# Starting the conversion of the second layer's weights at the third expert block instead of the first

## The chip, the core and the metric

One NeuronCore of one Trainium2 chip runs the whole program. The metric is device microseconds (us) of one execution. Engines are named as in the profile: PE is TensorE's matmul (PEld its weight load), DVE is VectorE, ACT is ScalarE, POOL is GpSimd, and SP is SyncE, which only issues transfers here.

## The reference

Three layers follow each other: a windowed attention with sink tokens, a mixture of eight experts, and a dense layer with a rational activation.

```
x = attention(q, k, v)                    # 1536 tokens x 512
for e in range(8):                        # each token goes to its best expert, or to none
    h = max(x[e's tokens] @ w1[e], 0)     # 512 -> 1024
    y[e's tokens] = gate * (h @ w2[e])    # 1024 -> 512
x = x + y
h = x @ w_in                              # 512 -> 2048, w_in in float64
g = (a0 + a1 h + a2 h^2 + a3 h^3) / (1 + |b0| |h| + |b1| h^2 + 1e-6)
out = g @ w_out                           # 2048 -> 512, w_out in float64
```

`w_in` and `w_out` arrive as 64-bit floats, 8 MB each. [...] The text below calls the dense layer "the second layer".

## The kernel before

**Stages.** The attention and the routing take the first 149 us. Then come nine expert blocks, 0 to 8 (eight experts and one spare block), each for up to 128 tokens. Then the second layer runs in 48 steps to the end.

**An expert block.** Block i needs its tokens transposed in SBUF (tile `xbT`, copied by ACT from PSUM, `block_tx_out`, L955) and eight weight chunks of 512 KB (tile `wch`, four of `w1` and four of `w2`). PE multiplies in two halves (`block_g1`, L965), ACT takes the positive part of each half (tile `hT`, L970), PE transposes the next block's tokens (tile `xtr`, L950) and multiplies by `w2` in eight pieces (`block_g2`, L976, sum `yps`). ACT copies the sum out and issues its store (L983, L984). From block 4 on, PE also transposes tokens of the second layer (`ztr`, L1046), which ACT and DVE split into a high and a low part (L1048, L1049).

**Weight chunks and their rooms.** 36 chunks (experts 0 to 3 and half of expert 4) have rooms of their own and are issued before block 1 begins. The chunks after them reuse twelve rooms, so each is issued once PE has used up the chunk that held its room. SP issues all of them (L606, L609) in the order in which the program lists them; an issue that has to wait holds up everything behind it on SP.

**The conversion.** One piece of `w_in` or `w_out` (128x512 values, 512 KB, tile `raw`) passes through these stations, one letter each in the order string:

```python
def conv_load():     # SP: L906, into one of three raw buffers
    sp.dma_start(r.rearrange("p a b -> p (a b)").bitcast(mybir.dt.int64), src)
def conv_word():     # T, DVE: L930, L931, L932, from raw into ta
def conv_hi(eng):    # U, ACT: L912, the high part
    eng.copy(chi[0][1], chi[0][0])
def conv_lo():       # V, DVE: L918, the low part
    dve.tensor_tensor(lo, v_, hi.bitcast(F32), op=ALU.subtract)
def loads_on():      # L
    more_chunks()
    while len(craw) < CRAW and conv_load():    # CRAW = 3 pieces ahead
        pass
```

24 of the 32 pieces (`NCM = 24`) belong to the expert blocks; the other eight are converted in the second layer. From the seventh piece on, a piece goes into a room that an expert's chunk has left.

**Order.** Nothing schedules the work at run time: each engine takes its instructions in program order. `BLOCK` (L72 to L75) is the order of one block. A word is a letter, a piece number and an offset to the block, so that `x01` in block i makes the transposes of block i+1.

```python
BLOCK = """
L2-1 G00 b03 L3-1 a00 o00 T00 U00 G10 V00 L40 x01 a10 T10 U10 F00 L50 F10 X01 V10 T20 U20 F20 F30 V20 L60 T30 U30
F40 F50 V30 z00 F60 F70 y00 L70
"""
```

G and F are PE's two products, a is `hT`, x and X the transposes and their copy, y the output, z the second layer's tokens, L the loads. T, U and V each stand four times, so a block has four places for a conversion. The table `bstep` (L1112 to L1117) maps the letters to functions. After the blocks, a branch over a loop (L1333) leads into the second layer; block 8's second product lies behind it, interleaved with the first steps.

Of the kernel before, what the change touches and what calls it, by code (L numbers as in the profile page):

```python
# [24 lines left out]
T = S // 128  # L25
# [48 lines left out]
F40 F50 V30 z00 F60 F70 y00 L70  # L74
"""  # L75
PO = (6, 12)


def build(nc, tc, q, k, v, n_sink, window, w_skip, w_gate, w1, w2, w_in, w_out, pa, pb, out):
    ctx = ExitStack()  # L80
    with ctx:
        ctx.enter_context(tc.manual_schedule())
        emit(nc, tc, ctx, q, k, v, n_sink, window, w_skip, w_gate, w1, w2, w_in, w_out, pa, pb, out)


def emit(nc, tc, ctx, q, k, v, n_sink, window, w_skip, w_gate, w1, w2, w_in, w_out, pa, pb, out):
    act, dve, pool, pe, sp = nc.scalar, nc.vector, nc.gpsimd, nc.tensor, nc.sync
# [822 lines left out]
    def conv_hi(eng):  # L910
        if chi:
            eng.copy(chi[0][1], chi[0][0])  # L912
            clo.append(chi.pop(0))

    def conv_lo():
        if clo:
            v_, hi, lo, into, key = clo.pop(0)
            dve.tensor_tensor(lo, v_, hi.bitcast(F32), op=ALU.subtract)  # L918
            into[key] = (hi, lo)

    def conv_word():

        if not craw:
            return [lambda: None] * 3
        r, *to = craw.pop(0)
        w0, w1_ = r[:, :, 0], r[:, :, 1]
        ta = stg_now[0].tile([128, 512], I32, tag="ta", name="ta", bufs=3 if stg_now[0] is stg else 2)
        chi.append((ta.bitcast(F32), *to))
        return [
            lambda: dve.tensor_scalar(ta, w1_, 3, 0x3FFFFFFF, op0=ALU.logical_shift_left, op1=ALU.bitwise_and),  # L930
            lambda: dve.scalar_tensor_tensor(ta, w1_, -0x40000000, ta, op0=ALU.bitwise_and, op1=ALU.bitwise_or),  # L931
            lambda: dve.scalar_tensor_tensor(ta, w0, 29, ta, op0=ALU.logical_shift_right, op1=ALU.bitwise_or),  # L932
        ]
# [82 lines left out]
    def place_out(ts):  # L1016

        for t in ts:
            w = scatter(pd[:, :], posi[:, t:t + 1], pk[:, t, :])
            tc.declare_no_dep(w.ins, group="pd", reason="every token has a place of its own")  # L1020
            tc.add_to_no_dep_group("pd", w.ins)
# [41 lines left out]
    def loads_on():  # L1063
        more_chunks()
        while len(craw) < CRAW and conv_load():
            pass

    def at_block(i):

        if i == 0:  # L1070
            flex.append(block_index(flex_sel, exk[:, 0:1], rt, ptr, ""))
        if i < 2:
            place_out(range(PO[0] * i, PO[i]))
        if i == 2:
            place_in()
        if i == 3:
            place_split()
            for t in range(XBUF):
                zx[t] = z_load(t)
# [27 lines left out]
    def step_z(i, n):  # L1107
# [4 lines left out]
    bstep = {  # L1112
        "G": step_G, "a": step_a, "F": step_F, "y": step_y,
        "b": step_b, "x": step_x, "X": step_X, "z": step_z,
        "T": lambda i, n: [op() for op in conv_word()], "U": lambda i, n: conv_hi(act), "V": lambda i, n: conv_lo(),
        "L": lambda i, n: loads_on(), "o": lambda i, n: at_block(i),
    }  # L1117
    made = set()
# [1 line left out]
    for p in range(-1, NBLK + 1):  # L1120
        for w in BLOCK.split():
            o, n, i = w[0], int(w[1]), p + int(w[2:])
# [236 lines left out]
    for w in JOIN.split():  # L1359
        o, n, i = w[0], int(w[1]), int(w[2:])  # L1360
# [17 lines left out]
    for n in range(-2, NS + 8):  # L1378
        for w in STEP.split():
            o, i, t = w[0], int(w[1]), n + int(w[2:])  # L1380
# [100 lines left out]
```

## Time and profile before

| what | value |
|---|---|
| median of 3 runs | 613.36 us (613.06 to 613.96) |
| the profiled execution | 612.33 us, span 610.5 us |
| PE / PEld busy | 537.9 us (88%) / 441.0 us (72%) |
| DVE / ACT / POOL busy | 415.5 / 351.9 / 261.1 us |
| moved by DMA | 86.59 MB, mean 142 GB/s |
| by SP's queue and its like (q1) | 72.75 MB |

The span is what the instructions cover; the profiled execution's own time is 1.83 us longer. Busy time alone doesn't tell what bounds a stage: PE is 88% busy over the whole span, yet there are stretches in which it does nothing. In each row of the timelines below the columns are start, duration, engine, line, operation and tiles, count, and in brackets how long the engine had been idle before and what ended that. SPq and ACTq rows are the issue of a transfer, not its landing.

### The profile page before, as it was taken

How to read it: one execution, taken by the hardware profiler on the slowest of the kernel's cores; microseconds unless marked ns; L12 is line 12 of the kernel's file. 1: busy time of each engine (PE TensorE's matmuls, PEld its weight loads, DVE VectorE, ACT ScalarE, POOL GpSimd, SP SyncE). 2: the span in 40 equal slices, each digit the busy share in tenths (PEclk: the TensorE clock that was granted, in tenths of full speed). 3: DMA queues.
4: the chain of work that ended last, by engine and by line, in shares of the span. 5: the costliest groups of instructions: out<-in, count | busy, mean ns of one | idle time of the engine just before them, and what ended most of it. 6: DMA issues, size and time to landing. Idle time of an engine off the chain costs nothing. (4 is left out here: it accounts for less than half of the span.)

```text
span 610.5 us, 8951 instructions
## 1 busy us (share of the span) xinstructions
PE 537.9 (88%) x2980; PEld 441.0 (72%) x2980; DVE 415.5 (68%) x842; ACT 351.9 (58%) x706; POOL 261.1 (43%) x347
## 2 busy tenths in 40 slices
PE   1899999984909999999699776999999999999993
PEld 1799999973608677777567555787888888888882
DVE  2698899987117277650038999877688776688761
ACT  3799999951003133331145656776777776677761
POOL 3865555325610020100023544766656634754453
PEclk9999999995968999999889999899999999999998
DMA  4929999647987957999302320101100100100001
GB/s 118 208 48 260 274 293 272 237 167 252 304 215 274 367 210 242 383 403 338 124 0 88 103 86 1 52 18 52 71 0 19 51 1 0 70 1 2 0 1 69
DMA packets 78599, 86.59 MB, mean 142 GB/s; under 512 B 43516, under 2 KB 56832, under 8 KB 78544
## 3 DMA queue, kind: packets, MB, share of 16 engines
q1 hardware_dynamic: 73312, 72.75, 38.1%
q0 software_dynamic: 3792, 10.80, 5.7%
q10 hardware_dynamic: 1440, 2.36, 1.0%
q8 instruction: 27, 0.44, 0.3%
q14 instruction: 28, 0.23, 0.1%
HBM read 74.61 MB, written 11.29 MB: 141 GB/s over the span
## 5 line engine op out<-in xcount | busy, mean ns | idle before, releaser
L1181 PE MATMUL hT<-zh,wc 128*128 128x512 f32 x384 | 132.5, 407 | 9.5 <-DMA raw<-in_moe_w_in 5.8
L1233 PE MATMUL acc<-wc,gh 128*128 128x512 f32 x368 | 94.0, 396 | 8.7 <-ACT gh L1201 8.7
L1206 POOL TENSOR_TENSOR w<-w,u 128x512 f32<-128x512 f32 x46 | 63.7, 1385 | 74.7 <-ACT w L1192 73.1
L1181 PEld LDWEIGHTS hT<-zh,wc 128*128 128x128 f32 x384 | 74.2, 193 | 27.0 <-issue 6.5
L1233 PEld LDWEIGHTS acc<-wc,gh 128*128 128x128 f32 x368 | 69.0, 189 | 26.6 <-ACT gh L1201 11.2
L965 PEld LDWEIGHTS hps<-xbT,wch 128*128 128x128 f32 x576 | 71.3, 205 | 21.3 <-ACT xbT L955 18.2
L965 PE MATMUL hps<-xbT,wch 128*128 128x128 f32 x576 | 71.9, 289 | 16.7 <-ACT xbT L955 16.7
L1209 POOL TENSOR_TENSOR gl<-p,gh 128x512 fp32r<-128x512 f32 x46 | 59.8, 1301 | 41.6 <-issue 32.3
L1181 PE MATMUL hT<-zl,wc 128*128 128x512 f32 x192 | 77.0, 401 | 0.4 <-DVE zl L1049 0.4
L912 ACT CAST wc<-ta 128x512 fp32r<-128x512 f32 x32 | 19.8, 618 | 84.2 <-DVE ta L932 72.7
L976 PE MATMUL yps<-wch,hT 128*128 128x512 f32 x144 | 64.5, 594 | 1.4 <-ACT hT L970 1.4
L1219 DVE SCALAR_TENSOR_TENSOR w<-w,cf,u 128x512 f32<-128x512 f32 x46 | 38.4, 834 | 32.2 <-ACT u L1198 32.2
L1233 PE MATMUL acc<-wc,gl 128*128 128x512 f32 x184 | 50.5, 393 | 0.2 <-POOL gl L1209 0.2
L378 ACT ACTIVATE P<-P,rmin 128x260 f32<-128x260 f32 (+1 forms) x96 | 48.6, 513 | 0.2
L1223 DVE SCALAR_TENSOR_TENSOR p<-p,cf,w 128x512 f32<-128x512 f32 x46 | 47.1, 1024 | 1.6
L976 PEld LDWEIGHTS yps<-wch,hT 128*128 128x128 f32 x144 | 26.3, 190 | 29.9 <-issue 26.7
L445 PE MATMUL xps<-P,vph 128*128 128x256 f32 x176 | 46.2, 294 | 0.0
L761 POOL DMA_INDIRECT zx<-xd,tix x12 | 12.9, 1075 | 75.3 <-PE ztr L1046 60.6
L1181 PEld LDWEIGHTS hT<-zl,wc 128*128 128x128 f32 x192 | 37.3, 194 | 9.4 <-DVE zl L1049 0.9
L1201 ACT CAST gh<-p 128x512 fp32r<-128x512 f32 x46 | 28.3, 615 | 26.9 <-DVE p L1223 26.7
L1196 ACT ACTIVATE u<-w,cf 128x512 f32<-128x512 f32 x46 | 33.3, 723 | 16.5 <-POOL w L1206 16.5
L1215 DVE TENSOR_TENSOR p<-p,hT 128x512 f32<-128x512 f32 x46 | 31.4, 682 | 14.2 <-ACT p L1194 14.2
(228 smaller groups left out, 1144.7 us busy)
## 6 DMA issues: line engine op xcount, KB each, us to landing
wch<-in_moe_w SPq DMA_DIRECT2D x72, 512.0 KB
raw<-in_moe_w_in SPq DMA_DIRECT2D x16, 512.0 KB
raw<-in_moe_w_out SPq DMA_DIRECT2D x16, 512.0 KB
kraw<-in_k SPq DMA_DIRECT2D x31, 192.0 KB
qraw<-in_q SPq DMA_DIRECT2D x8, 384.0 KB
vraw<-in_v SPq DMA_DIRECT2D x8, 384.0 KB
xd<-xs SPq DMA_DIRECT2D x16, 192.0 KB
yd<-zero SPq DMA_DIRECT2D x10, 256.0 KB
```

Source lines behind the costliest of these rows:

```text
L378: act.activation(dst, dst, AF.Exp, scale=-1.0, bias=rmin[u][:, t:t + 1], accum_out=ssum[:, u, t:t + 1])
L445: pe.matmul(xps[pr][bank][:, q0:q0 + w], vv, pp, start=(h == 0 and kt in (0, 3) and n == 0), stop=(h == 1 and kt == T - 2 and n == 2),)
L965: pe.matmul(ps[:, j * 128:(j + 1) * 128], w[c][:, f:f + 128], xb[:, c, :], start=(c == 0), stop=(c == KC - 1))
L976: pe.matmul(y, hT[f // 4][:, (f % 4) * 128:(f % 4) * 128 + 128], w, start=(f == 0), stop=(f == KF1 - 1))
L1181: pe.matmul(ps, ww, zz[:, k_, :], start=(i == 0), stop=(i == 3 * KC - 1))
L1196: act.activation(u, w, AF.Ln, bias=one6)
L1206: pool.tensor_tensor(w, w, u, op=ALU.mult)
L1209: pool.tensor_tensor(gl, p, gh.bitcast(F32), op=ALU.subtract)
L1215: dve.tensor_tensor(p, p, h2[n], op=ALU.mult)
L1219: dve.scalar_tensor_tensor(w, w, one6, u, op0=ALU.add, op1=ALU.mult)
L1223: dve.scalar_tensor_tensor(p, p, a0, w, op0=ALU.subtract, op1=ALU.mult)
L1233: pe.matmul(acc[g, m], ww[:, m * 128:(m + 1) * 128], oo, start=(f == 0 and i == 0), stop=(f == KF2 - 1 and i == 2))
```

## The change

A constant `CONV0 = 2` is added, and the letters T, U and V do nothing in blocks below it. The loads (`L`) are left as they are, so the first three pieces are still fetched at the first place; as no piece is used up before block 2, the fourth is not fetched before that either.

```diff
 PO = (6, 12)
+CONV0 = 2
...
-        "T": lambda i, n: [op() for op in conv_word()], "U": lambda i, n: conv_hi(act), "V": lambda i, n: conv_lo(),
+        "T": lambda i, n: [op() for op in conv_word()] if i >= CONV0 else None,
+        "U": lambda i, n: conv_hi(act) if i >= CONV0 else None, "V": lambda i, n: conv_lo() if i >= CONV0 else None,
```

PE's and POOL's orders stay the same. On DVE, ACT and SP the following moves. (The line numbers in the changed kernel are one or two higher.)

ACT's queue in blocks 0 and 1, from the copy of block 0's tokens on, before:

```order
L955 COPY xbT<-xtr 128x512
L970 ACTIVATE hT<-hps 128x512 x2
L912 CAST wc<-ta 128x512
L955 COPY xbT<-xtr 128x512
L912 CAST wc<-ta 128x512 x2
L983 COPY ys<-yps 128x512
L984 DMA yd<-ys 128x512
L970 ACTIVATE hT<-hps 128x512
L912 CAST wc<-ta 128x512
```

and now, up to the first conversion, which stands in block 2:

```order
L956 COPY xbT<-xtr 128x512
L971 ACTIVATE hT<-hps 128x512 x2
L956 COPY xbT<-xtr 128x512
L984 COPY ys<-yps 128x512
L985 DMA yd<-ys 128x512
L971 ACTIVATE hT<-hps 128x512 x2
L956 COPY xbT<-xtr 128x512
L984 COPY ys<-yps 128x512
L985 DMA yd<-ys 128x512
L971 ACTIVATE hT<-hps 128x512
L913 CAST wc<-ta 128x512
```

The copy of block 1's tokens (`xbT`) no longer stands behind a conversion. Six of the 24 conversions stood in blocks 0 and 1; the others keep their places in the order, each with a piece that is six earlier, and six are added at the end of block 6 and in block 7.

SP's queue from the last chunks with rooms of their own on, before:

```order
L606 DMA wch<-in_moe_w 128x1024 x4
L906 DMA raw<-in_moe_w_in 128x512 x4
L906 DMA raw<-in_moe_w_out 128x512
L609 DMA wch<-in_moe_w 128x2x512 x2
L906 DMA raw<-in_moe_w_out 128x512
L609 DMA wch<-in_moe_w 128x2x512 x2
L606 DMA wch<-in_moe_w 128x1024 x4
L609 DMA wch<-in_moe_w 128x2x512 x2
L906 DMA raw<-in_moe_w_out 128x512 x2
```

and now:

```order
L607 DMA wch<-in_moe_w 128x1024 x4
L907 DMA raw<-in_moe_w_in 128x512 x3
L610 DMA wch<-in_moe_w 128x2x512 x4
L607 DMA wch<-in_moe_w 128x1024 x4
L610 DMA wch<-in_moe_w 128x2x512 x2
L1025 DMA pb<-pd 128x12x3
L907 DMA raw<-in_moe_w_in 128x512
L907 DMA raw<-in_moe_w_out 128x512 x4
```

The ten chunks that complete expert 4 and begin expert 5 move ahead of the fourth piece.

SP's queue ahead of the branch, before:

```order
L609 DMA wch<-in_moe_w 128x2x512
L1129 TENSOR_LOAD rare
L1129 ISA x2
L1333 COMPARE_AND_BRANCH
L1333 UNCONDITIONAL_BRANCH x2
```

and now:

```order
L610 DMA wch<-in_moe_w 128x2x512
L907 DMA raw<-in_moe_w_out 128x512
L1131 TENSOR_LOAD rare
L1131 ISA x2
L1335 COMPARE_AND_BRANCH
L1335 UNCONDITIONAL_BRANCH x2
```

The last piece is fetched behind expert 8's last chunk; before, 14 chunks stood behind the last piece.

## Rows read from the trace of the kernel before

**Rows 1.** Stretches: us, PE, PEld, DVE, ACT, POOL busy (count), PEclk, DMA share, GB/s.

```profile
180.00:185.00 5.00, 2.00 (x9) 2.00 (x10) 4.15 (x7) 1.10 (x2) 0.00 (x0) 0.50 0.49 184
200.00:210.00 10.00, 10.00 (x75) 8.72 (x74) 0.33 (x1) 1.18 (x2) 1.01 (x1) 1.00 1.04 410
245.00:260.00 15.00, 15.00 (x89) 11.02 (x89) 10.24 (x17) 5.12 (x9) 2.63 (x3) 1.00 1.03 386
260.00:275.00 15.00, 14.84 (x88) 10.85 (x87) 8.15 (x15) 4.99 (x9) 0.68 (x2) 1.00 1.03 403
275.00:290.00 15.00, 15.00 (x90) 11.11 (x89) 0.80 (x2) 2.84 (x5) 1.10 (x2) 1.00 0.93 338
242.00:282.00 40.00, 39.84 (x243) 29.90 (x242) 21.14 (x35) 11.91 (x21) 4.50 (x4) 1.00 1.03 391
```

**Rows 2.** PE's timeline over the blocks.

```profile
159.92 7.03 PE L976 MATMUL yps<-wch,hT 128*128 128x512 f32 x16
183.00 10.28 PE L965 MATMUL hps<-xbT,wch 128*128 128x128 f32 x64 [16.05 <-ACT xbT L955]
...
212.80 3.70 PE L976 MATMUL yps<-wch,hT 128*128 128x512 f32 x8 [1.20 <-ACT hT L970]
216.34 7.31 PE L965 MATMUL hps<-xbT,wch 128*128 128x128 f32 x64
...
223.92 7.03 PE L976 MATMUL yps<-wch,hT 128*128 128x512 f32 x16
230.79 7.31 PE L965 MATMUL hps<-xbT,wch 128*128 128x128 f32 x64
...
245.68 7.31 PE L965 MATMUL hps<-xbT,wch 128*128 128x128 f32 x64
...
268.46 5.42 PE L976 MATMUL yps<-wch,hT 128*128 128x512 f32 x12 [0.16 <-ACT hT L970]
...
290.76 7.31 PE L965 MATMUL hps<-xbT,wch 128*128 128x128 f32 x64
303.89 0.80 PE L1181 MATMUL hT<-zh,wc 128*128 128x512 f32 x1 [5.82 <-DMA raw<-in_moe_w_in]
```

**Rows 3.** ACT's timeline around that wait.

```profile
181.84 0.62 ACT L912 CAST wc<-ta 128x512 fp32r<-128x512 f32 x1 [18.88 <-DVE ta L932]
182.37 0.58 ACT L955 COPY xbT<-xtr 128x512 f32<-128x512 f32 x1
```

**Rows 4.** DVE's timeline, the first piece and the start of the second.

```profile
179.93 0.43 DVE L930 TENSOR_SCALAR ta<-raw 128x512 int32<-128x512 int32 x1 [22.49 <-DMA raw<-in_moe_w_in]
...
183.10 0.42 DVE L930 TENSOR_SCALAR ta<-raw 128x512 int32<-128x512 int32 x1
```

**Rows 5.** SP's issues: the first piece, the nineteenth, and two in block 5.

```profile
161.67 0.33 SPq L906 DMA_DIRECT2D raw<-in_moe_w_in  x1
...
240.32 0.34 SPq L906 DMA_DIRECT2D raw<-in_moe_w_in  x1
...
252.34 1.92 SPq L609 DMA_DIRECT2D wch<-in_moe_w  x4
256.31 0.82 SPq L906 DMA_DIRECT2D raw<-in_moe_w_out  x2
```

**Rows 6.** DVE's timeline, a piece of block 5 that came late.

```profile
263.89 0.43 DVE L930 TENSOR_SCALAR ta<-raw 128x512 int32<-128x512 int32 x1 [3.70 <-DMA raw<-in_moe_w_out]
...
267.07 0.68 DVE L1049 TENSOR_TENSOR zl<-ztr,zh 128x512 fp32r<-128x512 f32 x1
```

**Rows 7.** ACT's timeline behind that piece.

```profile
265.81 0.62 ACT L912 CAST wc<-ta 128x512 fp32r<-128x512 f32 x1 [6.34 <-DVE ta L932]
...
267.43 0.34 ACTq L984 DMA_DIRECT2D yd<-ys  x1
267.81 0.60 ACT L970 ACTIVATE hT<-hps 128x512 f32<-128x512 f32 x1 [0.41 <-PE hps L965]
```

**Rows 8.** The chain that ended last: start, duration, what; one transfer.

```profile
326.67 3.14 DMA raw<-in_moe_w_in
```

## The prediction

> **What bounds the kernel now.** I read PE's timeline first, because PE is busy in nearly every stretch and only its gaps can be won. In the expert blocks the large gap stands at 183.00: 16.05 us, ended by ACT's copy of block 1's tokens [rows 2]. ACT's timeline then shows why that copy is late: ahead of it in ACT's order stands the first conversion, for which ACT waited 18.88 us until 181.84; the copy follows at 182.37 [rows 3]. DVE's timeline shows the step before: DVE waited 22.49 us for the first piece, until 179.93 [rows 4]. SP had issued that piece at 161.67 [rows 5]. So PE stands still because a piece that no expert needs comes late, and ACT takes its work in order. A second price stands beside it: the granted clock is 1.00 at 200 to 210 but 0.50 (the lower level, 1.2 GHz) at 180 to 185, behind the gap [rows 1], and block 1's first product takes 10.28 us where the same 64 matmuls take 7.31 [rows 2].
>
> **What is removed.** Block 0's products end at 159.92 + 7.03 = 166.95, and block 8 begins at 290.76 [rows 2], 123.81 us for blocks 1 to 7. A block without second-layer tokens takes 230.79 - 216.34 = 14.45 us, one with them 245.68 - 230.79 = 14.89 [rows 2]. Three of the one and four of the other are 102.9 us. So the most that can go is **20.9 us**: 16.05 for the gap, 2.97 (10.28 - 7.31) for the low clock, 1.20 for the wait at 212.80, also behind a late piece, and 0.7 in small waits. The words, casts and differences of 24 pieces stay the same in number and length; they only move.
>
> The new cover is block 2 to block 7. One piece takes DVE and ACT 183.10 - 179.93 = 3.17 us together [rows 4], four pieces 12.7 us of a block's 14.45 or 14.89. DVE and ACT can hold that pace. What can fail is the arrival of pieces.
>
> **What comes back, 1: the fourth piece.** It now stands behind ten weight chunks on SP, which PE frees during block 1. After the first piece lands at 179.93, pieces two and three, the ten chunks and the fourth piece have to land: 13 transfers of 0.524 MB, and by an estimate 1 MB of block inputs and outputs, 7.9 MB. At 410 GB/s (200 to 210) that takes 19.2 us, at 338 GB/s (275 to 290) 23.3 us [rows 1], so it lands at 199.1 to 203.3. Three DVE operations and one cast later, and after a 0.60 us activation, block 3's `hT` is out; from the late piece at 263.89 to the cast's end at 266.43 [rows 6, 7] are 2.5 us, so that is 202.2 to 206.4. PE wants it at 166.95 + 2 x 14.45 + 7.58 (223.92 - 216.34) = 203.4 [rows 2]. The stall is 0 to 3.0 us; I take 1.5, the middle, as each end is a measured rate.
>
> **What comes back, 2: blocks 5 to 7.** From 242 to 282 the DMA share is already 1.03 at 391 GB/s [rows 1], while the last pieces and the chunks of experts 6 to 8 are loaded. The change moves about six and a half more pieces into that stretch: 19 had been issued by 242, from 161.67 to 240.32 [rows 5], and now, at four a block with three fetched ahead, there are 12 or 13. They are 3.4 MB, 8.7 us at 391 GB/s. The price is at least nothing, since the stretch from 282 on is not full (275 to 290 moves 338 GB/s) and chunks are loaded ahead of their use; it is at most 8.7 us. How close it runs is shown by the late piece in block 5: DVE waited 3.70 us, ACT's cast 6.34 us, block 6's `hT` came at 267.81, and PE lost 0.16 us [rows 6, 7, 2]. A piece later than that costs PE what it is later. The same pattern now comes in blocks 5, 6 and 7. I take 2.0, nearer to the lower end, since the row with the same pattern lost 0.16.
>
> Here stands the rule that speaks most against the change. The rows first: 386, 403 and 391 GB/s over 15, 15 and 40 us [rows 1]. The Trainium skill, "DMA: Bandwidth & Descriptors", section "Bandwidth", says that for transfers between HBM and SBUF the core's share of HBM, about 358 GB/s, is the limit; by it the 15.6 MB of that stretch and the 3.4 MB would take 53.1 us instead of 40, the upper end would be 13.1 us, and the time about 602 us, which is the second rival's ground. The trace disagrees with that limit: it moves 403 GB/s over 15 us.
>
> **What comes back, 3: the branch.** The last piece is issued behind expert 8's last four chunks, in block 7. In block 5 such a piece, behind four chunks, was issued 256.31 - 245.68 = 10.6 us after the block's start, and landed 18.2 us after it, at 263.89 [rows 2, 5, 6]. DVE's last operation behind it ended 3.9 us later (267.07 + 0.68) and ACT issued the block's output 3.9 us later (267.43 + 0.34) [rows 6, 7]: 22.1 us after the block's start. PE ends block 8's first product 14.89 + 7.31 = 22.2 us after it [rows 2]. That is a tie, so the bound below is nothing. If the branch waits for the last output to land, one lone transfer's 3.14 us [rows 8] is the bound above. I take 2.0, the upper half, because a late piece adds to it. PE's 5.82 us behind the branch [rows 2] I leave as it is.
>
> **Sum.** -20.9 + 1.5 + 2.0 + 2.0 = -15.4 us, from the profiled 612.33 us to 596.9. The median of the runs lies 1.03 us above the profiled one: **598.0 us**.
>
> **Rivals.**
> - *Nearly all is kept.* Pieces land in time, and less than 3 us come back: 592.5 to 595.5. For it: 410 GB/s at 200 to 210, and the tie at the branch. Against it: three places at which a piece is just in time.
> - *The transfers set the pace.* The terms come near their upper ends, 3.0 + 8.7 + 3.1 = 14.8 us, or 9 to 15 in all: 601.5 to 607.5. For it: a share of 1.03 over 40 us [rows 1]. Against it: expert 8's second half isn't needed until after the branch.
> - *Slower: three pieces per landing time.* There are three buffers, so 24 pieces need eight rounds of landing time plus some 1.9 us of DVE's words, from about 182 on. A landing of 12.7 us makes 8 x 14.6 = 117, which ends with the present branch at about 299; beyond that the kernel is slower. At 14.2 us it ends 12 us later, at 625. For it: the first piece took 18.3 us (161.67 to 179.93) [rows 4, 5]. Against it: at full DMA share a piece took 263.89 - 256.31 = 7.6 us [rows 5, 6].
> - *No effect.* The copy comes early, but expert 1's chunks hold PE at the same place. Then 613.4. Against it: in SP's order they stand before those of experts 2, 3 and 4, and all of these before the first piece.
>
> **How the numbers follow.** Forecast, with 3 to 9 us coming back: 0.52. Nearly all kept: 0.23. The transfers set the pace: 0.19. No effect: 0.03. Slower: 0.03. A measurement of this kernel can tell about 0.2%, 1.2 us, from no change. So faster is 0.52 + 0.23 + 0.19 = 0.94, same 0.03, slower 0.03. The range from 593 to 605 holds the forecast (595.5 to 601.5) and most of the two cases beside it; it leaves out the best half microsecond, the worst of the full-queue case and the last two cases.
>
> **What would show it.** PE's timeline should have no gap between block 0 and block 1, the first product of block 1 should take 7.3 us at a granted clock of 1.00, and block 3 should begin near 196. Step 1 is right if PE waits for `hT` in block 3 near 203 to 206, behind a cast that waits for the fourth piece. Step 2 is right if DVE waits for pieces in blocks 5 to 7 at a DMA share of 1, and PE's gaps there stay near 2 us in sum. Step 3 is right if DVE or ACT is the last to reach the branch, with block 8's first product ending near 279. A gap of many microseconds that ends with a chunk (`wch`) rather than with ACT would make the prediction wrong, and so would a DMA rate under 300 GB/s while pieces are outstanding.

## The result, and the profile after

The changed kernel took 598.6 us (median of four runs, 596.64 to 600.03) against 613.21 us before: a ratio of 0.976 (95% interval 0.973 to 0.979), faster by 14.6 us where 15.4 were forecast. Measured twice more, on two different chips, it gave 0.986 (0.983 to 0.989) and 0.982 (0.979 to 0.985). So the change is worth 1.4 to 2.4%, and part of the question is why it differs.

The profiled run of after took 598.66 us, its span 596.9. PE's timeline over the blocks answers to [rows 2].

```profile
166.77 4.14 PE L966 MATMUL hps<-xbT,wch 128*128 128x128 f32 x34
171.74 0.27 PE L966 MATMUL hps<-xbT,wch 128*128 128x128 f32 x1 [0.83 <-issue]
172.45 0.36 PE L966 MATMUL hps<-xbT,wch 128*128 128x128 f32 x1 [0.44 <-issue]
173.14 5.02 PE L966 MATMUL hps<-xbT,wch 128*128 128x128 f32 x28 [0.32 <-issue]
...
185.30 7.31 PE L966 MATMUL hps<-xbT,wch 128*128 128x128 f32 x64
...
199.75 7.31 PE L966 MATMUL hps<-xbT,wch 128*128 128x128 f32 x64
...
253.52 5.42 PE L977 MATMUL yps<-wch,hT 128*128 128x512 f32 x12 [1.79 <-ACT hT L971]
260.93 7.31 PE L966 MATMUL hps<-xbT,wch 128*128 128x128 f32 x64
...
270.09 5.42 PE L977 MATMUL yps<-wch,hT 128*128 128x512 f32 x12 [1.42 <-ACT hT L971]
277.50 7.31 PE L966 MATMUL hps<-xbT,wch 128*128 128x128 f32 x64
290.57 0.80 PE L1183 MATMUL hT<-zh,wc 128*128 128x512 f32 x1 [5.76 <-ACT hT L971]
```

The gap of 16.05 us is gone: block 1 follows block 0. Blocks 1 to 7 take 277.50 - 166.77 = 110.7 us instead of 123.8; with nothing in their way they would take 102.9. What is left, 7.8 us, lies in two places. Block 1 takes 185.30 - 166.77 = 18.53 us, 4.1 too many: from 171 on PE stopped three times, 1.6 us in all, for nothing that the profile shows ("issue"). Blocks 6 and 7 lose 3.7 us behind `hT`. Block 3, where the forecast had a stall, takes 14.45 us.

The same stretches of after by windows (columns as in [rows 1]):

```profile
171.00:173.00 2.00, 0.63 (x2) 0.37 (x2) 0.00 (x0) 0.00 (x0) 0.52 (x1) 1.00 0.93 280
173.00:178.00 5.00, 4.86 (x29) 4.87 (x30) 0.00 (x0) 0.60 (x1) 0.00 (x0) 0.66 0.94 215
200.00:210.00 10.00, 10.00 (x75) 8.57 (x74) 6.80 (x13) 2.91 (x6) 3.16 (x3) 1.00 0.76 274
242.00:282.00 40.00, 36.78 (x225) 27.61 (x224) 21.90 (x36) 10.69 (x19) 3.85 (x3) 1.00 0.99 383
```

After the stop the granted clock fell below 1.00 (0.66 as a mean from 173 to 178). So of the 4.1 us the stop itself is 1.6, and 2.5 are the slower matmuls behind it. From 242 to 282 the DMA share is 0.99, against 1.03 before [rows 1]. SP's issues show what stands ahead of the late pieces of blocks 6 and 7, and DVE's timeline how long it waits for them:

```profile
235.76 2.03 SPq L610 DMA_DIRECT2D wch<-in_moe_w  x4
239.67 0.34 SPq L907 DMA_DIRECT2D raw<-in_moe_w_out  x1
240.10 0.38 SPq L907 DMA_DIRECT2D raw<-in_moe_w_in  x1
240.58 0.86 SPq L607 DMA_DIRECT2D wch<-in_moe_w  x2
...
251.27 3.20 SPq L610 DMA_DIRECT2D wch<-in_moe_w  x4
258.78 0.34 SPq L907 DMA_DIRECT2D raw<-in_moe_w_in  x1
```

```profile
201.51 0.43 DVE L931 TENSOR_SCALAR ta<-raw 128x512 int32<-128x512 int32 x1 [3.87 <-DMA raw<-in_moe_w_in]
...
248.95 0.43 DVE L931 TENSOR_SCALAR ta<-raw 128x512 int32<-128x512 int32 x1 [5.05 <-DMA raw<-in_moe_w_out]
...
265.50 0.43 DVE L931 TENSOR_SCALAR ta<-raw 128x512 int32<-128x512 int32 x1 [3.20 <-DMA raw<-in_moe_w_in]
```

In both places a piece is issued behind four chunks, and DVE waits 5.05 and 3.20 us for it: the pattern of [rows 5, 6]. The DVE row at 201.51 is the landing of the fourth piece. The piece issued at 240.10 is the seventeenth, and the chunks at 240.58 are the 57th and 58th of 72.

### The profile page after: what moved, and what is told of

Same layout as the page of the kernel before. It is cut to its first block, busy times and chain, and to the rows that moved or that the text cites. A ratio compares the mean times of both kernels' runs of the same rounds, so it can differ in the third digit from the quotient of the medians.

```text
span 596.9 us, 8944 instructions
## 1 busy us (share of the span) xinstructions
PE 536.4 (90%) x2980; PEld 439.3 (74%) x2980; DVE 415.1 (70%) x842; ACT 352.0 (59%) x706; POOL 261.5 (44%) x347
## 4 chain that ended last, share of the span: by engine, by line
PE 34%; DVE 9%; ACT 3%; issue 2%; POOL 2%; DMA 1%; POOLq 0%; ACTq 0%; DVEq 0%
PE hT L1183 17%; PE acc L1235 16%; DVE w L1221 2%; DVE p L1225 1%; DVE w L1223 1%; DVE p L1219 1%; DVE ta L933 1%; DVE ta L932 1%; DVE wc L919 1%; DVE p L1217 1%; ACT u L1198 1%; DMA raw<-in_moe_w_in 1%; POOL w L1208 1%; ACT u L1200 1%; POOL early L1208 0%
## 5 line engine op out<-in xcount | busy, mean ns | idle before, releaser
L1235 PEld LDWEIGHTS acc<-wc,gh 128*128 128x128 f32 x368 | 68.8, 188 | 26.5 <-ACT gh L1203 11.2
L966 PEld LDWEIGHTS hps<-xbT,wch 128*128 128x128 f32 x576 | 69.0, 199 | 7.1 <-issue 5.6
L966 PE MATMUL hps<-xbT,wch 128*128 128x128 f32 x576 | 70.0, 283 | 2.3 <-issue 1.6
L931 DVE TENSOR_SCALAR ta<-raw 128x512 int32<-128x512 int32 x32 | 14.0, 438 | 44.1 <-DMA raw<-in_moe_w_in 34.1
L919 DVE TENSOR_TENSOR wc<-ta,wc 128x512 fp32r<-128x512 f32 x32 | 27.6, 863 | 23.1 <-ACT wc L913 22.4
```

The source lines that it names most:

```text
L966: pe.matmul(ps[:, j * 128:(j + 1) * 128], w[c][:, f:f + 128], xb[:, c, :], start=(c == 0), stop=(c == KC - 1))
L1235: pe.matmul(acc[g, m], ww[:, m * 128:(m + 1) * 128], oo, start=(f == 0 and i == 0), stop=(f == KF2 - 1 and i == 2))
```

## The experiments

Times are medians; ratios are to the kernel before on the same chip. "Ideal" for blocks 1 to 7 is 102.9 us, for blocks 6 and 7 together 29.78.

| kernel | time | ratio (95%) | blocks 1-7 | block 1 | block 3 | blocks 6+7 |
|---|---|---|---|---|---|---|
| change | 598.6 | 0.976 (0.973-0.979) | 110.7 | 18.53 | 14.45 | 33.5 |
| the change, second time | 604.56 | 0.986 (0.983-0.989) | 114.8 | 14.45 | 21.14 | 34.9 |
| the change, third time | 601.5 | 0.982 (0.979-0.985) | 113.8 | 14.45 | 20.56 | 34.6 |
| from block 1 | 607.09 | 0.990 (0.987-0.993) | 117.9 | 25.85 | 14.45 | 32.9 |
| from block 3 | 602.61 | 0.982 (0.979-0.985) | 106.5 | 14.45 | 14.45 | 33.3 |
| pieces before chunks | 601.33 | 0.980 (0.978-0.981) | 112.7 | 14.45 | 19.27 | 34.7 |
| scatters later | 603.66 | 0.984 (0.982-0.985) | 113.2 | 14.45 | 21.01 | 33.5 |
| four raw buffers | 593.41 | 0.967 (0.964-0.969) | 104.4 | 14.45 | 15.90 | 29.8 |
| four raw buffers, second time | 593.14 | 0.969 (0.966-0.973) | 103.7 | 14.44 | 15.23 | 29.8 |
| before, four raw | 612.97 | 0.999 (0.998-1.000) | 123.8 | | | |
| cast on DVE | 607.72 | 0.990 (0.987-0.994) | 119.2 | 14.45 | 14.45 | |
| cast on DVE, four raw | 603.94 | 0.986 (0.982-0.990) | 114.8 | 14.45 | 14.45 | |
| four raw, one slot less | 592.10 | 0.965 (0.964-0.966) | 104.4 | 14.45 | 15.98 | 29.8 |

**Conversion from block 1 or from block 3.** `CONV0 = 1`, and `CONV0 = 3`.

> Conversion begins with block 1 instead of block 2. My theory (the first piece lands near 180 whatever the order says, and ACT takes its work in order): block 1's first cast waits until about 182, ACT's activation of block 1's second half and the copy of block 2's tokens stand behind it, and PE gets a gap of 5 to 8 us near 180 to 187, ended by ACT; the pieces of blocks 5 to 7 come one block earlier, so at most the 3.7 us that blocks 6 and 7 lose there come back. Sum 600 to 603 us. Rival (transfers set the pace, so every piece begun earlier is a gain): no gap from ACT near 182, blocks 6 and 7 at 14.9 us each, 594 to 596 us.

> Conversion begins with block 3; four pieces are then left and are converted between block 7 and the branch. My theory (PE needs about 5.8 us behind block 8's first product in any case, and only what DVE and ACT are late beyond that costs): four pieces take 4 x 3.17 = 12.7 us of DVE and ACT after block 7, against 7.3 us of product, and they must land first, so DVE and ACT come to the branch 6 to 10 us after PE's product instead of 1.6 us and the branch is 4 to 9 us later: 603 to 608 us. Rival (DVE, ACT and SP are covered by something longer at the branch): within 1.5 us of the change, 597 to 600 us.

From block 1, PE's timeline has the gap that the theory places there, in block 1, ahead of the half of its second product that needs the second `hT`:

```profile
186.98 5.47 PE L977 MATMUL yps<-wch,hT 128*128 128x512 f32 x8 [8.07 <-ACT hT L971]
```

The time, 607.09, lies 4 us above the expected range. The first piece landed at 183.9, not near 180, so the gap, 8.07 us, is at the upper end of the 5 to 8 expected; the low clock behind it was not counted (5.47 us for a half product that takes 3.70 at full clock, as in [rows 2]). About half of the 4 us is not in these rows: the profiled run was the fastest of the four, 605.08. From block 3, blocks 1 to 5 are whole; PE's and DVE's rows at the branch show what four pieces behind block 7 cost:

```profile
294.12 0.79 PE L1183 MATMUL hT<-zh,wc 128*128 128x512 f32 x1 [13.35 <-DVEq L1335]
```

```profile
293.01 0.06 DVE L1141 MEMSET cf<- 128x1 f32 x1
```

PE waits 13.35 us instead of 5.76, and starts 1 us after DVE's last operation before the branch. PE waits 5.3 to 5.8 us there where DVE is early, so by these rows, as an estimate, the branch hides DVE up to some 4 us behind PE's product; beyond that each microsecond counts. The time, 602.61, lies just under the expected range. So the later start trades a whole block 3 for a late branch. Its ratio, 0.982, lies inside what three measurements of the change gave (0.976 to 0.986), so it is not shown that block 2 is a better start than block 3. Against block 1 (0.990, 0.987 to 0.993) all three measurements of the change lie lower, the nearest by 0.4%, where the intervals still touch.

**Pieces before chunks.**

```diff
 def loads_on():
-    more_chunks()
     while len(craw) < CRAW and conv_load():
         pass
+    more_chunks()
```

> In each place where loads are issued, second-layer pieces are issued before the expert chunks instead of behind them; the same bytes. My theory (the gaps of blocks 6 and 7 come from pieces that stand behind up to four chunks on SP): DVE's waits for pieces in blocks 5 to 7 (5.05 and 3.20 us) fall under 1 us, PE's gaps before the second-half products of blocks 6 and 7 (1.79 and 1.42 us) go, 594.5 to 595.5 us. Rival (the DMA's rate is the limit, so what a piece gains a chunk loses): PE waits for a chunk (wch) instead, or the blocks' lengths stay near 17 us, 597.5 to 600 us.

The gaps stayed (DVE waits 5.20 and 4.39 us). The time, 601.33 us, lies a little above the rival's range, so the run looks like the rival. But SP's issues show that the edit did not do what it says at the places that matter:

```profile
236.82 1.93 SPq L610 DMA_DIRECT2D wch<-in_moe_w  x4
241.19 0.34 SPq L907 DMA_DIRECT2D raw<-in_moe_w_out  x1
```

The four chunks still go first. With three buffers, all taken, no piece can be issued at that place in the program, whatever stands first in the code. The run tells the theories apart only together with the next.

**Four raw buffers.** A fourth `raw` buffer, four pieces fetched ahead; room for it comes from the tiles `ta` (three buffers to two) and `ys` (two to one). PE, DVE, ACT and POOL keep their order.

```diff
-CRAW = 3
+CRAW = 4
...
-        r = stg_now[0].tile([128, 512, 2], I32, tag="raw", name="raw", bufs=3 if stg_now[0] is stg else 2)
+        r = stg_now[0].tile([128, 512, 2], I32, tag="raw", name="raw", bufs=4 if stg_now[0] is stg else 2)
...
-        ta = stg_now[0].tile([128, 512], I32, tag="ta", name="ta", bufs=3 if stg_now[0] is stg else 2)
+        ta = stg_now[0].tile([128, 512], I32, tag="ta", name="ta", bufs=2 if stg_now[0] is stg else 2)
...
-        ys = mo.tile([128, DM], F32, tag="ys", name="ys", bufs=2)
+        ys = mo.tile([128, DM], F32, tag="ys", name="ys", bufs=1)
...
```

> Four buffers for raw pieces instead of three, four pieces fetched ahead; the rows of PE, DVE, ACT and POOL stay in the same order, only SP's pieces move ahead of chunks: the fourth piece is issued with the first three near 167 instead of behind ten chunks. My theory (a piece costs what it is late, and it is late because its buffer comes free too late and SP then has chunks ahead of it): no hT gap in block 3, DVE's waits in blocks 5 to 7 under 2 us, PE's gaps in blocks 6 and 7 (3.7 us) gone, 592 to 595 us. Rival (the DMA's rate sets the pace): PE waits for chunks (wch) or the gaps of blocks 6 and 7 stay, 597 to 600 us.

593.41 us. PE's timeline, SP's issues and two windows of this kernel, and one window of the change (first profile) over the same two blocks:

```profile
209.91 3.70 PE L977 MATMUL yps<-wch,hT 128*128 128x512 f32 x8 [1.18 <-ACT hT L971]
...
258.12 7.31 PE L966 MATMUL hps<-xbT,wch 128*128 128x128 f32 x64
...
273.00 7.31 PE L966 MATMUL hps<-xbT,wch 128*128 128x128 f32 x64
285.61 0.80 PE L1183 MATMUL hT<-zh,wc 128*128 128x512 f32 x1 [5.30 <-DMA raw<-in_moe_w_in]
```

```profile
165.82 8.21 SPq L907 DMA_DIRECT2D raw<-in_moe_w_in  x4
```

```profile
241.00:256.00 15.00, 15.00 (x90) 11.05 (x89) 10.63 (x18) 5.65 (x10) 1.51 (x1) 1.00 1.03 404
256.00:271.00 15.00, 15.00 (x91) 11.12 (x90) 8.79 (x14) 4.50 (x9) 1.00 (x1) 1.00 1.04 402
```

```profile
242.00:277.00 35.00, 31.78 (x183) 22.92 (x182) 20.72 (x35) 10.06 (x18) 3.21 (x3) 1.00 1.03 399
```

The fourth piece goes out with the first three. Blocks 6 and 7 lose nothing, at the same full DMA share and the same rate, 404 and 402 GB/s, against 399 in the change, which loses 3.7 us there. The DMA's rate was not what held PE there; it was the order in which SP asked for things, and the buffer that set it. DVE still waited 3.26 us for one piece, until 264.75, at no cost to PE. Block 3 still lost 1.45 us (the gap of 1.18); that is taken up under "One slot less". The Trainium skill gives a limit of about 358 GB/s for a core ("DMA: Bandwidth & Descriptors", section "Specifications"); the rows of this kernel, too, lie above it. The Trainium skill also says, on the same page in the section "Bandwidth", that each core gets about that when both cores of a pair stream; here one core runs the program.

**The fourth buffer without the change, and the four-buffer kernel again.** `CONV0 = 0` with four buffers; and a repeat.

> The kernel before (conversion from the first block) with four buffers for raw pieces: the fourth buffer without the change. My theory (the 16 us gap is the landing of the first piece, which no buffer brings forward, against ACT's order): the gap at 183 stays at 15 to 22 us, 608 to 615 us. Rival (too few buffers were the whole fault, and the later start is not needed): the gap is gone, 593 to 600 us.

> Four buffers for raw pieces, a second time. It gave 593.41 us (593.1 to 593.8) with a first piece at 185.6 us. My theory (with four buffers a late first piece is covered, so the time hangs little on the chip's DMA): 592 to 595 us whatever the changed kernel beside it does. Rival (it was a good chip): 596 to 600 us, or as far below the changed kernel as the cost of its block 3 alone.

```profile
185.37 9.39 PE L966 MATMUL hps<-xbT,wch 128*128 128x128 f32 x64 [17.59 <-ACT xbT L956]
```

Alone, the buffer is worth nothing (0.999): in its profile, to which the row belongs, the first piece landed at 182.29 and ACT's copy stood behind it, as in [rows 3, 4]. The change alone gives 1.4 to 2.4%, both together 3.1 to 3.3%. Of the repeat's six runs five took 592.6 to 594.2 us and one 599.63; that one was not profiled and stays unexplained.

**The cast on DVE.** The kernel before (conversion from block 0), with the cast of the blocks moved, with three buffers and with four. Against the changed kernel:

```diff
-CONV0 = 2
+CONV0 = 0
...
-            eng.copy(chi[0][1], chi[0][0])
+            eng.tensor_copy(chi[0][1], chi[0][0]) if eng is dve else eng.copy(chi[0][1], chi[0][0])
...
-        "U": lambda i, n: conv_hi(act) if i >= CONV0 else None, "V": lambda i, n: conv_lo() if i >= CONV0 else None,
+        "U": lambda i, n: conv_hi(dve) if i >= CONV0 else None, "V": lambda i, n: conv_lo() if i >= CONV0 else None,
```

> The kernel before (conversion from the first block), with the pieces' cast on DVE instead of ACT; no block step of ACT then stands behind a piece. My theory (the 16 us gap came from ACT's order alone): DVE still waits for the first piece until about 180, but PE has no gap at 183, block 1 begins near 167, blocks 1 to 7 take 14.5 to 14.9 us, and DVE's 24 pieces of 3 to 3.3 us end 275 to 288: 592 to 597 us. Rival (a late piece holds PE in another way too, by DVE's differences for the tokens' second halves or by SP's chunks): the gap only moves, 603 to 613 us.

> Both: conversion from the first block, the cast on DVE, and four buffers for raw pieces. If a late piece costs only through ACT's order, the fourth buffer adds nothing to the cast on DVE: within 1 us of that kernel, 592 to 597 us. If pieces also run late for the branch, it is 2 to 4 us faster than that kernel.

The first half of the theory held: DVE waited for the first piece until 184.56, and PE ran blocks 1, 2 and 3 at 14.45 us each. The first piece had stopped PE only through ACT's order. The second half fell: 607.72 us, inside the rival's range, and by one of the two ways that the rival named, SP's chunks. PE now waits for tokens and chunks, and SP's issues show why:

```profile
227.53 1.11 PE L1047 MATMUL ztr<-ident,zx 128*128 128x128 f32 x4 [4.14 <-DMA zx<-xd,tix]
...
252.27 0.79 PE L966 MATMUL hps<-xbT,wch 128*128 128x128 f32 x2 [2.38 <-DMA wch<-in_moe_w]
```

```profile
222.44 9.77 SPq L907 DMA_DIRECT2D raw<-in_moe_w_out  x4
234.92 0.33 SPq L907 DMA_DIRECT2D raw<-in_moe_w_in  x1
235.30 0.95 SPq L610 DMA_DIRECT2D wch<-in_moe_w  x2
```

DVE is a block behind. Each piece on SP waits for a buffer that DVE still holds, and the chunks behind it, which the four-buffer kernel above issues at 220.56, go out at 235.30. The places that POOL needs for its token loads stand behind the pieces on DVE as well (POOL waited for them until 224.10). The wait moved from ACT's queue to SP's and DVE's. With four buffers the same kernel took 603.94 us, 3.8 us less: the second of the two cases expected, but PE waited for chunks there too (4.14 us inside the first product of block 6), so it was chunks, not the branch, that ran late.

**The stop in block 1, and the change again.**

```diff
-if i < 2:
-    place_out(range(PO[0] * i, PO[i]))
+if i == 0:
+    place_out(range(0, 6))
 if i == 2:
+    place_out(range(6, 12))
+if i == 3:
     place_in()
-if i == 3:
+if i == 4:
     place_split()
```

> The second six scatters of places are issued in block 2 instead of block 1, the loads that read the places in block 3, the token loads in block 4. Theory: in block 1 PE stood still and then ran at the lower clock (4.1 us in all) with no wait but issue, while those scatters filled the queues; without them block 1 takes 14.5 us, and since PE is then 4.1 us earlier it waits about 2 us for block 3's hT behind the fourth piece: 595.5 to 597.5 us, and if the scatters do the same wherever they are, block 2 takes 17 to 19 us instead. Rival (the stop is not theirs: it comes with any full DMA or with the place in the code): block 1 still takes 17 to 19 us, 598 to 600 us.

> The changed kernel once more, beside the next three on one chip. If the stop of PE in block 1 (issue, then the lower clock: 4.1 us in the changed kernel, 0.45 us and no low clock with conversion from block 1, none with conversion from block 3 or with pieces ahead of chunks) belongs to the program, block 1 takes 18.5 us again and block 3 has no gap. If it comes and goes, block 1 takes 14.45 us and block 3 gets a gap of 3 to 5 us that ends with hT, behind the fourth piece, as in the two kernels without the stop. Either way 597 to 601 us.

> The changed kernel a third time, beside the next three on one chip. Two measurements of it gave 0.976 and 0.986 of the kernel before. My theory: what differs is when the first pieces land (181.9 us in the first, 186.0 in the second), and with them the fourth (201.5, 204.9) and whether PE waits for it in block 3 (no gap, 4.76 us); so a first piece at 182 or before goes with a block 3 of 14.5 to 17 us and 597 to 600 us, one at 184 to 186 with a block 3 of 19 to 21 us and 601 to 606 us. Rival (the difference lies elsewhere, in PE's clock or the second layer): the blocks from 167 to 290 take the same time in both cases.

With the scatters later the time was 603.66 us, above both ranges. There was no stop; but in two more profiles of the unchanged program there was none either, so that run says nothing of the cause. The stop came in the change's first profile and, shorter (0.45 us), with conversion from block 1. What it is stays open. What takes its place is shown by the change's second profile, PE, DVE and ACT:

```profile
209.02 8.79 PE L977 MATMUL yps<-wch,hT 128*128 128x512 f32 x16 [4.76 <-ACT hT L971]
...
273.26 7.11 PE L977 MATMUL yps<-wch,hT 128*128 128x512 f32 x12 [2.57 <-ACT hT L971]
```

```profile
186.04 0.43 DVE L931 TENSOR_SCALAR ta<-raw 128x512 int32<-128x512 int32 x1 [28.14 <-DMA raw<-in_moe_w_in]
...
204.93 0.43 DVE L931 TENSOR_SCALAR ta<-raw 128x512 int32<-128x512 int32 x1 [9.30 <-DMA raw<-in_moe_w_in]
```

```profile
206.85 0.62 ACT L913 CAST wc<-ta 128x512 fp32r<-128x512 f32 x1 [11.94 <-DMA raw<-in_moe_w_out]
207.37 0.58 ACT L984 COPY ys<-yps 128x512 f32<-128x512 f32 x1
207.98 0.34 ACTq L985 DMA_DIRECT2D yd<-ys  x1
208.37 0.60 ACT L971 ACTIVATE hT<-hps 128x512 f32<-128x512 f32 x1 [0.42 <-ACT ys L984]
```

The fourth piece lands at 204.93, `hT` ends at 208.97, and PE had wanted it at 204.26: a gap of 4.76 us. The product behind it takes 8.79 us instead of 7.03 to 7.13, at a granted clock of 0.58 from 209 to 213. The third profile has the same rows (first piece 185.05, fourth 203.85, gap 4.29). In the first profile the stop in block 1 had made PE 4.1 us late, so the fourth piece, landed at 201.51, was in time: `hT` was out at 205.55, and PE began the product at 207.33. Had PE not stopped, it would have wanted `hT` at about 203.3 and waited about 2.3 us, an estimate from these numbers. The first piece's landing alone does not set the fourth's: with the scatters later the first landed at 180.58 and the fourth at 204.75, and block 3 took 21.01 us.

**One slot less.** Four buffers, and the first conversion of block 2 left out: `if (i, n) > (CONV0, 0)` in the places of `if i >= CONV0`.

> Four buffers, and the first of block 2's four conversions left out, so that 23 stand in blocks 2 to 7 and one before the branch. My theory: the 1.45 us that block 3 still loses with four buffers come from the fifth piece (landed 206.8, behind ten chunks), which stood before the activation PE waits for; now it stands behind it, so block 3 takes 14.45 us, and the piece at the branch costs nothing, because DVE came there at 278.3, 2 us before PE ended block 8's product: 591 to 592.5 us, 0.5 to 2 us under four buffers alone. Rival (the branch has no room left): block 3 is won, and as much or more is lost at the branch, 592.5 to 596 us.

592.10 us (591.6 to 593.24), 1.0 us under four buffers on the same chip, with ranges that overlap, and not for the reason given: block 3 still took 15.98 us, and PE's and DVE's rows name another wait:

```profile
207.78 3.70 PE L977 MATMUL yps<-wch,hT 128*128 128x512 f32 x8 [1.26 <-ACT hT L971]
...
284.83 0.79 PE L1183 MATMUL hT<-zh,wc 128*128 128x512 f32 x1 [6.11 <-DVEq L1335]
```

```profile
204.55 0.17 DVE L1028 CAST yix<-pb 128x12 int32<-128x12 f32 x1 [8.15 <-DMA pb<-pd]
```

DVE waits for the places (`pb`), and the conversions, the cast and `hT` stand behind that. The same wait stands in the two four-buffer profiles, 6.91 us until 205.51 and 6.23 us until 204.10; the fifth piece, which the theory blamed, came 1.0 us behind it. At the branch DVE's last operation ended at 283.78, 5.1 us behind PE's product, and PE's wait grew to 6.11 us: the branch had no room left, as the rival said. In its profile the stretch from block 1's start to the second layer took 118.4 us, against 116.5 with four buffers; block 1 merely began 1.5 us earlier (166.44 against 167.91). The 1.0 us is not explained by the edit. Both versions beat the change and the kernel before.

## Why the prediction was right, and where not

*What bounds the kernel, and the 20.9 us.* Right. In every kernel with conversion from block 2 on, block 1 follows block 0, its product takes 7.31 us where PE did not stop, and with late pieces covered blocks 1 to 7 take 103.7 to 104.4 us: 19.4 to 20.1 of the 20.9 are had. That the first piece reached PE through ACT's order, and in no other way, is shown by the cast on DVE: the piece came as late, and the gap was gone.

*Comes back, 1 (1.5 us, 0 to 3.0).* The place was right, the size wrong: 0 in the first profile, 21.14 - 14.45 = 6.7 and 6.1 us in the next two. Three things were mis-sized. The base: the first piece was taken to land at 179.93, as in [rows 4]; it landed at 181.9, 186.0 and 185.1. The transfers from there to the fourth piece took 19.7, 18.9 and 18.8 us, close to the lower end of the 19.2 to 23.3 that were reckoned. The chain behind it: 2.5 us to the cast's end were copied from block 5, and 0.6 added for the activation, 3.1 in all; but at this place the output's copy and store stand between cast and `hT`, and it takes 208.97 - 204.93 = 4.04 us. And the clock: the low clock behind a gap was counted in what goes (2.97 us), but not in what comes back, where it took 1.7 us.

*Comes back, 2 (2.0 us, 0 to 8.7).* Right in the place and the wait (PE behind `hT`, behind a late piece), too small, and wrong in its working. It cost 3.7, 5.2 and 4.8 us in blocks 6 and 7, the last two with 1.7 us of low clock in block 7. The upper end rested on six and a half more pieces behind 242, of which 12 or 13 would have been issued by then. SP had issued 17, against 19 before, and 58 chunks, against 50 before. So the change left fewer transfers for that stretch, not 3.4 MB more, and the core moved 383 GB/s from 242 to 282, against 391 [rows 1]. Even by the prediction's own block times, blocks 2 to 5 with their 16 conversions end at 166.95 + 3 x 14.45 + 1.5 + 2 x 14.89 = 241.6. What cost PE was the order of the issues, not more bytes. At the lower end, the row that was leaned on, 0.16 us lost in block 5 [rows 2], had all but no slack left, and one case with no slack does not stand for three blocks. Four buffers remove the whole term at an unchanged DMA rate.

*Comes back, 3 (2.0 us, 0 to 3.1).* Nothing came. DVE and ACT did reach the branch last (DVE's last operation ended at 286.4, PE's product at 284.8), as forecast. But PE's 5.82 us [rows 2] were taken as a cost that adds to theirs, and they run beside it: with DVE 2 us ahead of PE the wait was 5.30 us (four buffers), with DVE 1.6 behind it 5.76 (the change), with DVE 5.1 behind it 6.11 (one slot less), with DVE 12.3 behind it 13.35 (from block 3).

*Not foreseen.* The stop in block 1, 4.1 us, in one of three profiles. In the kernel before, that stretch lay under the gap.

*The sum.* In the first profile 4.1 + 0 + 3.7 + 0 = 7.8 us came back against 5.5 forecast; 20.9 - 7.8 = 13.1 is the 13.3 us by which the second layer starts earlier (303.89 - 290.57) but for 0.2 at block 0. The other 1.3 us of the 14.6 lie outside the blocks: 0.3 us in the span behind the start of the second layer, and the rest in how the two profiled runs stand to their medians. In the second and third profiles 11.9 and 10.9 us came back. So 598.0 was near the first measurement partly by luck: a stop that nobody foresaw took the place of the wait in block 3 that was forecast, and 1.3 us outside the blocks made up for part of the rest. Over the three measurements the gain was 14.6, 8.8 and 11.8 us.

*The rivals.* By its number, "the transfers set the pace" (9 to 15 us back, 601.5 to 607.5) came true in the second and third measurements; its mechanism is refuted by the four buffers. The rule that spoke most against the change was priced at about 602, which adds only the 4.4 us between the two upper ends; with its own upper end of 13.1 us the sum would be 609. "Slower: three pieces per landing time" did not come; the real danger of that kind, pieces that hold up chunks on SP, appeared only with the cast on DVE. "Nearly all kept" is what four buffers give: 593. One sign that was to make the prediction wrong did show, a DMA rate under 300 GB/s while pieces are outstanding (215 from 173 to 178 in the first profile, 228 from 170 to 180 in the second). It was a poor sign: from 170 to 180 the kernel before moved 232.

## What to carry to other kernels

Work that waits for a late transfer holds up whatever stands behind it on the same engine, so ask for each engine and each DMA queue what that is; here moving the wait from ACT to DVE gave back most of what it won. When a start is delayed until data is there, look at the next thing that has to arrive at the new, earlier time, and at the buffer that decides when it is asked for: here the fourth buffer was worth nothing before the change and 8.4 and 11.2 us after it (601.5 to 593.14, 604.56 to 593.41). A forecast that counts a low clock behind a removed gap has to count it behind the new gaps too.

## What the runs showed of the hardware

While six scatters of 128 rows of three values each are under way, the core's transfers run slower. In the change's second profile they are issued from 165.1 to 171.5, with the scatters later from 176.8 to 183.6, and there they take about 10 us (9.7 to 11.1) from issue to landing. The window from 170 to 180 of the first, then of the second, in which they have only begun to be issued, and the next ten microseconds of the second:

```profile
170.00:180.00 10.00, 10.00 (x61) 7.37 (x60) 0.00 (x0) 1.67 (x3) 3.01 (x3) 1.00 1.04 228
```

```profile
170.00:180.00 10.00, 10.00 (x59) 7.30 (x58) 0.00 (x0) 1.67 (x3) 3.64 (x4) 1.00 1.02 386
180.00:190.00 10.00, 10.00 (x75) 8.65 (x74) 4.23 (x7) 2.47 (x5) 3.80 (x5) 1.00 1.11 286
```

The DMA share is full in all three, but the rate is 228 GB/s with them and 386 before they bear on it, and 286 where they went instead (322 there in the change's second profile). The Trainium skill has a rule of this direction ("DMA: Bandwidth & Descriptors", section "Specifications": transfers below 512 bytes do not reach the line rate); the trace agrees, and adds the price for the large transfers beside them, some 1.6 MB in 10 us. Moving the scatters bought nothing: the fourth piece landed at 204.75, as late as without.

Three measurements of the changed kernel differed by 6 us (598.6 to 604.56), those of the kernel before beside them by 0.2 (613.21 to 613.39). The first piece landed between 181.9 and 186.0 in the profiles of the one program; why it varies was not tried.
